# Warm transposes moved to a PSUM bank of their own, and attention's order and engine tables replaced

## The chip, the cores and the metric

The kernel runs on one core of a Trainium2 chip. The metric is the device time of one execution in microseconds (us), as the median of several runs. Five engines work side by side, each through a queue of its own in order: TensorE (PE: matmuls, transposes), VectorE (DVE), ScalarE (ACT), GpSimd (POOL) and SyncE (SP, which issues DMAs).

## The reference

```python
scores = scale * np.matmul(q, k.transpose(0, 1, 3, 2))          # 4 batches x 8 heads, 576 x 576, head size 64
thresh = np.max(scores, axis=-1, keepdims=True) - tau
scores = np.where(scores >= thresh, scores, -1000000000.0)
scores = scores - np.max(scores, axis=-1, keepdims=True)
attn = np.exp(scores)
attn = attn / (np.sum(attn, axis=-1, keepdims=True) + 1e-09)
x = np.matmul(attn, v)                                          # to 2304 tokens x 512
...
x = (sigmoid(x @ w_gate) * (x @ w_val)) @ w_out                 # 512 -> 1536 -> 512
h = x @ w_in                                                    # 512 -> 2048
out = (h * np.cos(h)) @ w_out2
```

## The kernel before

Every fp32 matrix product is made from high and low parts (fp32r), so most operands are first split: a "hi" copy on ACT or POOL, a "lo" difference on DVE or POOL. The program has two stages. The first computes attention and, in between, part of the first MoE layer's products; the second holds the rest of both MoE layers. Its order is in the tables LATER and WHO, which the change does not touch.

Attention goes through 16 pairs of heads, `Pair` p, each with 9 tiles of 128 query rows, `Queries` n (144 tiles). A tile is a chain: **S** (scores, PE, into the PSUM tile `s`, of which there are two), **M** (row minimum of the negated scores, DVE), **E** (exponential, ACT), **Y** (threshold, one value per row, on ACT, POOL or DVE by the table YS), **K** (mask and row sum, DVE, which reads `s` a last time), **T** and **t** (transposes of the result, PE, into `t`), **H**/**h** (hi part, ACT), and the lo part in one of three ways by LOWS and LOWS_L: **L**/**l** (DVE, straight from PSUM), **C** and **G** (ACT copies, POOL subtracts), or **N**/**n** and **O**/**o** (PE subtracts, ACT copies). **V** multiplies with the values; **F** and **A** (ACT, DVE) fold its two halves, and SHARED says which V instead takes more matmuls and needs no fold. The splits of q, k and v are **Q q**, **J j**, **Z z** (capital for hi, small for lo), scaled by **s**; the engine of each, per pair, stands in WHERE, as do **X x** and **U** for attention's result. The twelve weight pieces of the first stage pass through **w** (ACT), **4** and **5** (bit operations on DVE, L516 and L519), **6** (ACT) and **7** (POOL). **P** are the MoE products that fill PE from the fourth pair on.

Who goes when is written out by hand in ORDER: one string of such letters for each engine, which `Plan.put_out` follows letter by letter. A wrong guess in such a string is paid for as a wait, since an engine takes nothing out of turn. `Plan.task` has a flag `alone` for the DVE operations that can't run beside one of POOL.

Before the first tile PE does 42 transposes of the identity into `warm`, a tile of the ring "v" (two PSUM banks, used later by V and P). Between the first tiles it does further groups of four, `filler` (letter **D**), 14 groups by the table FILL, which write a part of the tile's own `s` that nobody reads:

```python
    def filler(s):
        for _ in range(4):
            nc.tensor.transpose(s()[:, 1, HALF:HALF + P], ident, ident)
...
            for _ in range(int(FILL[n])):
                task("PE", 0.43, "D", lambda: filler(s), sc, uses=[s])
```

Of the kernel before, what the change touches and what calls it, by code (L numbers as in the profile page):

```python
# [52 lines left out]

ORDER = dict(
    PE=(
        "SDDSTDSDDDDSTStNnTSNTSDtnDTTSNNNStTDNStTSTVDDtNSSTVBTtSSTTDDNtVSSTTVNNtSTVtSNnSTTNVtSNSBTtSNSTnVTTVNtSnSTTNN"
        "SNtPTPtPSSPVTTPSVPtSTPSBPPtTPSTSPTPStVPTTSSPVNtPNSPTSVtPTTPStVPTPBSPTtPSTPSTtPVSTTVtSSVTtVnSTTPSPtPTPPBSStPP"
        "TPSTSVtTPSPSTTVPtSPTSVtTVTStPSPPTBPStSTPVTTPSStVTPTPSPtSPTPStPVTTSVPtTPBSPStTPPTSPPTStVTPSStTVPSPSVTtVSPTTPP"
        "tSSTPBPtTSSTTVtPSTTVStSTtVnVTSTPStPTPBSPtTPSPTVSSTtVPSSTTPPtPTSPStPTVTSPtSTBPPTPVStSPTPSPTtPSVTTSVtSPTPSVPTt"
        "PSStTVBPTPSSTtPVTPSStTVPTTPSPTPtSPTPVSPttSPTPBSPTVStTVSTTPSPtVTPSStPPTtPSSPTVPTTSSVtPTPSBPTPtSSPTPTPStPSVTTV"  # L60
        "tSSTVtPTTVtPSBTPSPPTStPSTTVStVTPSTPPStPPTPStSVTPTSPtSTVPTBPSTtSPtVTPSSVTTVPStPTPtPPTPTPtVPBBVV"
    ),
    ACT=(
        "JQJQEQHwEYEHEhOEHo6HOEhowEHHHOOOYEhhHEO6hpwCEEHYH6hOsHEERwhCHaaHHYEhE6OFwEHCHHEOOh6hEYHFhpwOoEHYEOYHh6OEREHw"
        "aOhFHCoY6EEHHFahwOoEHHHOOOhhEEH6wehEeFHCEp6HEYehFHERwYYEChHeeEH6HehEYYEFHCwHEYeEHOhOFhp6eHEYhFwCYHeHEh6FHREe"
        "HEYheHCYEhHEXFeHEHHFhhEQHhEYpoaFHCHhEeEHeREEhYCHeHeEEhHCFEeHHEHFphheCHEhHFEHhFCEEYRHheeECHEHHeFhCEYYEFHHHeQE"
        "YYhhEeHhYpeFHHCEFZhECeHREYHChEHeeEChYHYEHFeEYYHEHFhheEFHhEpFECHHheHEREhHCeHEHhFYeEHEHFHhhJHhEYFEoHFpHCEhYHeR"
        "EhHeYEEHeFEEhHFCHHHEEYehhpeHEheEHHFhHCYEeEReCHFEHhYEHhECeEFCHHHEFhHphECEFHhCehHEEFCRHHYYEEhFCHeYhHEEHHHFXsHe"
        "hEhHEepFhhEHeRCEHeEFYhCHEHHFCEheYEFCHhhEEYHeheHHEYEeFpHHCEhFEHReEHCheEEHHeheEEFHCHHhhFpHEhFCHHYhEeRFCHEECHhE"
        "eeHCHFhEFEHHHEehhYeEHChEEYFHHephHEEFHCRHChhYEEHeFEFHCFHHEhhEHYhCpeHHXhFeFbFX"  # L70
    ),
    DVE=(
        "jqjMqKqMLMKKM4MKY5KMLYMK4KM5MKllKMlM4Y5KKIMMYlLYKK4lMML5KKlMM4KA5MlKlKAM4M5KKlMIMYKK45MMAzKLKAM4YKM5MllKKLMM"
        "Yl4KA5MKLIKMlAMLKK4lM5KLMMLlKKAMM4K5lKAMlMLlK4A5ILKlMALYMKLKlMMlKLKMALKLMLAllMKLxKAMLMIlKKLMMKKMlLMKKlMAMKYL"
        "LKLAllMIMKlLAKlMAYMKKLMMYlKKLMMlAKKALLMLMKllMLlKALIMKYAlKMMKzlKMLMlKKLMMAKLKLAllMMYYKALlMYAIKKLlMMLKKlMMLKLl"
        "AMKLKLLllAMMLKAKMLAIMlKLKMLlMYKKLMMAKKlAMMLLLKKllMLIMlYKKLLlAMMKKMYMKLlAKMlMKKMALLYKAlMMlYYIKKAlMMlLYKKAzMML"
        "KKlMMAlLKKLLLAxMLlMKLYlKMYAIllKMMKLMKYlAKMYLAMlKKAMMYllKKLlLMMYLKKAMMLYYIKAlLMKYKMMlYYKLKMLlMKKALLMllAILYlAK"
        "MLlKMAMKKMlMYYKLAMKlKAMLLMLllKKMMlKKLLMAMlLIYKKAMMllYKKLMMAAKLLMAllKKlULILxlxAUAAUxx"
    ),
    POOL=(  # L80
        "YZYzJYjs7cYQqYJ7jG7QqZYGz7YcYGJ7jsQ7YUqZY7XxcUXxYsYG7YQq7GJjY7GscQZGYzJ7qG7UjGYZzYcsxYUXqYYJGYjZYYGzYscQGJYG"
        "YqUZGjYXGczGsUXxxqGGYJGjscGQqZzJjUYXYGYGcYxZUYXxjGYsQzqYYYcsQYqGJZGYzjGsYcYGGUQZGqYGJGjUYcGXxZzYQqJYGUjGGcsZ"
        "XxGQqUXGxzJsGjYYcGQqGYGYGGYZcJjYzYUGZYGGzUYYcGGXXRR"
    ),
    SP=(
        "100W21kkdd0W21sWsssk0kWdd1ssssW0rrssssWdkk2RRdWssssrrWRRk0kWssss12ddgWgg0ddssssWrgg1sssrsWggRRgkDk0ssss2dgrr"
        "ssssRRgggk21kd0gssssDDgkr1rdgssssRg2dRkggssss0grgdrRRsgsssD2ggdg1kkssss0rDrdg2ssssg1gdRRggD2kkdssssrr1RRssss"
        "kggk0dssssggg1rr0sRsgss2dRggdkkDD0ssgrdsskkssssd2rggR1Rssssrr2g0Rksssggks1DddgRssssd0grr2ggRkssssdggRk10dggr"
        "ssDssrgssssggkgd1kR2ssgssRDggDdrssssdk2rRRkgssssggrrssssRRDDDDggg"
    ),  # L90
)
# [1848 lines left out]
```

## Time and profile before

| | |
|---|---|
| median of 3 runs | 1111.09 us (1110.85 to 1112.88) |
| the profiled execution | 1111.66 us |
| its span, first to last instruction | 1109.9 us |
| busy: PE, DVE, ACT, POOL | 97%, 83%, 69%, 54% of the span |
| attention's last products on PE start | 401.18 us |
| granted TensorE clock, mean | 0.998 |

The profiled execution lies 0.6 us above the median, and 1.8 us of it are outside the span. Instructions are listed by engine, source line and the tiles they write and read. Matmuls overlap, so that their durations exceed the distance from one to the next.

### The profile page before, as it was taken

The page shows a single profiled execution, that of the slowest core. Times are in us where ns is not written, and L with a number is a line of the kernel's source. Part 1 is how long each engine was busy: PE and PEld are TensorE (multiplying, and loading weights), DVE is VectorE, ACT ScalarE, POOL GpSimd, SP SyncE. Part 2 cuts the span into 40 slices and gives each one's busy share as a digit, 9 for nine tenths or more (in the row PEclk, how much of TensorE's full clock was granted, in tenths as well). Part 3 has the DMA queues.
Part 4 walks back from the last instruction along what each step waited for, and adds up shares of the span by engine and source line. Part 5 has one row for each costly group of instructions (what it writes and reads, how often), then busy time and mean ns, then how long its engine had stood idle before and what let it go on. Part 6 is the DMA issues. An engine that isn't in the chain of part 4 may idle for free.

```text
span 1109.9 us, 17653 instructions
## 1 busy us (share of the span) xinstructions
PE 1076.6 (97%) x5816; PEld 917.4 (83%) x5816; DVE 926.6 (83%) x1631; ACT 766.7 (69%) x1507; POOL 597.3 (54%) x508
## 2 busy tenths in 40 slices
PE   6889999999999999999999999999999999999998
PEld 6768888888888878987888888888888888888886
DVE  6999998998998856887887655879788899889997
ACT  5889879888888855555654434357876767797774
POOL 4788878878886625432234442244244525445563
PEclk9999999999999999999999999999999999999999
DMA  6657675766666449898876645685444445457752
GB/s 184 158 154 217 193 211 167 199 181 187 182 188 182 125 163 313 303 322 293 292 259 219 200 172 197 219 254 209 157 169 168 152 152 190 173 207 240 279 211 85
DMA packets 88093, 225.53 MB, mean 203 GB/s; under 512 B 14410, under 2 KB 22722, under 8 KB 78274
## 3 DMA queue, kind: packets, MB, share of 16 engines
q1 hardware_dynamic: 87842, 224.08, 63.1%
q8 instruction: 46, 0.75, 0.3%
q10 hardware_dynamic: 160, 0.33, 0.1%
q14 instruction: 45, 0.37, 0.1%
HBM read 150.18 MB, written 59.84 MB: 189 GB/s over the span
## 4 chain that ended last, share of the span: by engine, by line
PE 51%; DVE 1%; DMA 1%; ACT 0%; issue 0%; ACTq 0%
PE h L1391 5%; PE h L1392 5%; PE h L1393 5%; PE h L1580 4%; PE h L1581 4%; PE h L1582 4%; PE o L1700 4%; PE o L1701 4%; PE o L1702 4%; PE o L564 3%; PE o L563 3%; PE o L565 3%; DMA early<-gd 1%; PE o L1791 1%; PE o L1790 1%; PE o L1792 1%
## 5 line engine op out<-in xcount | busy, mean ns | idle before, releaser
L1626 POOL TENSOR_TENSOR g<-raws,g 128x512 fp32r<-128x512 f32 x68 | 94.6, 1400 | 138.1 <-ACT g L1625 115.9
L915 DVE TENSOR_REDUCE sm<-s 128x1 f32<-128x576 f32 x144 | 106.1, 750 | 10.9 <-PE s L909 8.1
L923 DVE SCALAR_TENSOR_TENSOR p<-s,sm,p 128x576 f32<-128x576 f32 x128 | 102.6, 812 | 12.0 <-ACT p L920 7.6
L920 ACT ACTIVATE p<-s,sm 128x576 f32<-128x576 f32 x128 | 94.0, 742 | 15.3 <-DVE sm L915 10.6
L1391 PE MATMUL h<-x,w 128*128 128x256 f32 (+1 forms) x304 | 101.4, 333 | 0.0
L1392 PE MATMUL h<-x,w 128*128 128x256 f32 (+1 forms) x304 | 101.3, 333 | 0.0
L1393 PE MATMUL h<-x,w 128*128 128x256 f32 (+1 forms) x304 | 101.3, 333 | 0.0
L851 ACT ACTIVATE PT<-t 128x512 fp32r<-128x512 f32 (+1 forms) x160 | 86.2, 554 | 21.6 <-PE t L939 18.1
L909 PE MATMUL s<-kk,qh 128*128 128x288 f32 x320 | 92.0, 318 | 9.3 <-DVE p L923 7.8
L1006 PE MATMUL v<-PT,vn 128*128 128x320 f32 (+2 forms) x532 | 84.8, 303 | 3.2 <-DVE x L981 3.2
L1710 DVE TENSOR_TENSOR y<-o,y 128x512 f32<-128x512 f32 x120 | 78.7, 682 | 6.1 <-PE o L1702 5.8
L939 PE MATMUL t<-ident,p 128*128 128x128 f32 x512 | 76.3, 276 | 3.5 <-DVE PT L862 1.9
L1006 PEld LDWEIGHTS v<-PT,vn 128*128 128x128 f32 (+1 forms) x532 | 74.0, 187 | 5.6 <-DVE x L981 4.1
L871 POOL TENSOR_TENSOR PT<-praw,PT 128x512 fp32r<-128x512 f32 x48 | 64.1, 1336 | 26.5 <-ACT praw L866 15.6
L1700 PE MATMUL o<-g,w 128*128 128x512 f32 x196 | 76.7, 392 | 0.5 <-ACT o L1716 0.5
L1701 PE MATMUL o<-g,w 128*128 128x512 f32 x196 | 76.4, 390 | 0.0
L1702 PE MATMUL o<-g,w 128*128 128x512 f32 x196 | 76.3, 389 | 0.0
L909 PEld LDWEIGHTS s<-kk,qh 128*128 128x128 f32 x320 | 58.8, 189 | 21.1 <-DVE p L923 9.9
L1580 PE MATMUL h<-form,w 128*128 128x512 f32 x192 | 75.0, 390 | 0.5 <-ACT side L1549 0.5
L1581 PE MATMUL h<-form,w 128*128 128x512 f32 x192 | 74.8, 389 | 0.0
L1582 PE MATMUL h<-form,w 128*128 128x512 f32 x192 | 74.7, 389 | 0.0
L528 POOL TENSOR_TENSOR w<-wt,w 128x512 fp32r<-128x512 f32 x30 | 39.6, 1325 | 64.5 <-ACT w L524 64.4
(207 smaller groups left out, 3520.2 us busy)
## 6 DMA issues: line engine op xcount, KB each, us to landing
w<-wd SPq DMA_DIRECT2D x62, 1024.0 KB
wd<-stage SPq DMA_DIRECT2D x64, 512.0 KB
gd<-st SPq DMA_DIRECT2D x64, 256.0 KB
wraw<-in_moe_w_out_dram SPq DMA_DIRECT2D x28, 512.0 KB
raw_k<-in_k_dram SPq DMA_DIRECT2D x30, 304.0 KB
raw_q<-in_q_dram SPq DMA_DIRECT2D x30, 288.0 KB
wraw<-in_moe_w_in_dram SPq DMA_DIRECT2D x16, 512.0 KB
spare<-gd SPq DMA_DIRECT2D x7, 1024.0 KB
```

Of the source, the lines that this page charges most:

```text
L909: nc.tensor.matmul(s[:, half, 0:HALF], qq, keys[:, half * HALF:half * HALF + HALF], start=(i == 0), stop=(i == len(mms) - 1),)
L915: nc.vector.tensor_reduce(self.sm()[:, 0:1], self.s()[:, :, 0:HALF], axis=AX.XY, op=ALU.min)
L1006: nc.tensor.matmul(o, w, x, start=z == 0, stop=z == len(steps) - 1)
L1391: nc.tensor.matmul(o, w_hi, x(0, c), start=begin, stop=False, **late)
L1392: nc.tensor.matmul(o, w_hi, x(1, c), start=False, stop=False, **late)
L1393: nc.tensor.matmul(o, w_lo, x(0, c), start=False, stop=c == KC - 1, **late)
L1580: nc.tensor.matmul(ps(), of(0, c), hi, start=fresh and c == 0, stop=False, skip_group_check=True)
L1581: nc.tensor.matmul(ps(), of(0, c), lo, start=False, stop=False, skip_group_check=True)
L1582: nc.tensor.matmul(ps(), of(1, c), hi, start=False, stop=c == 1, skip_group_check=True)
L1700: nc.tensor.matmul(ps(), of(0, c), hi, start=begin, stop=False, skip_group_check=True)
L1701: nc.tensor.matmul(ps(), of(0, c), lo, start=False, stop=False, skip_group_check=True)
L1702: nc.tensor.matmul(ps(), of(1, c), hi, start=False, stop=True, skip_group_check=True)
```

## The change

The `filler` groups no longer write the tile's `s` but `warm`, which becomes a buffer of the ring "v" under the name `spare`; the first V is made to wait for all of them, since `spare` holds one of the ring's two banks until then. FILL has 15 groups instead of 14, all in the first five tiles; the opening block has 36 transposes instead of 42. All of ORDER is replaced, and so are LOWS, LOWS_L, SHARED, WHERE and YS. In counts over the first stage: Y on POOL 55 to 44, on ACT 50 to 38, on DVE 39 to 62; G 48 to 43; L 92 to 96, l 89 to 96; N 20 to 21, n 7 to 0; V without fold 5 to 6; on POOL J 14 to 9, Z 15 to 10, X 12 to 9, j 15 to 14, q 15 to 14, z 13 to 14; what leaves POOL of the hi copies goes to ACT, of the lo parts to DVE.

```diff
 ORDER = dict(
     PE=(
-        "SDDSTDSDDDDSTStNnTSNTSDtnDTTSNNNStTDNStTSTVDDtNSSTVBTt...
+        "SDDDSDSDDTTSNNSDTtDSTSNDDDtTSSTNNNDtDDTDSStNTTVNNtSSTVBT...
...
     DVE=(
-        "jqjMqKqMLMKKM4MKY5KMLYMK4KM5MKllKMlM4Y5KKIMMYlLYKK4lMML5...
+        "jqMjqKqMMKK45MMYYKKlMMYLKKlMM4q5lKKlMlM4j5KKMMlILYKKMl4M...
...
 FILL = (
-    "223002001 200002000 000000000 000000000 000000000 000000000 000000000 000000000 "
+    "444120000 000000000 000000000 000000000 000000000 000000000 000000000 000000000 "
...
     warm = ps_v.tile([P, 512], F32, tag="v", name="warm", bufs=2)
-    for _ in range(42):
+    for _ in range(36):
         nc.tensor.transpose(warm[:, 0:P], ident, ident)
...
-    def filler(s):
+    spare = buf("v", lambda: warm, 2, any_order=True)
+    fills = []
+
+    def filler():
 
         for _ in range(4):
-            nc.tensor.transpose(s()[:, 1, HALF:HALF + P], ident, ident)
+            nc.tensor.transpose(spare()[:, 0:P], ident, ident)
...
-                task("PE", 0.43, "D", lambda: filler(s), sc, uses=[s])
+                fills.append(task("PE", 0.43, "D", filler, sc, uses=[spare]))
...
-                      *lasts, pair.v_done, pvs[0], uses=[bank, self.PT, self.LZ, pair.vb])
+                      *lasts, pair.v_done, pvs[0], *(fills if pvs[0] is None else []), uses=[bank, self.PT, self.LZ, pair.vb])
```

How the instructions stand at two places. First PE's queue at the start of the program, before: `warm` is the opening block, `s` the scores, `s<-ident` the filler groups, `t` the transposes of a finished tile.

```order
L597 MATMUL warm<-ident 128x128 x42
L909 MATMUL s<-kk,qh_99 128x288
L909 MATMUL s<-kk,ql_101 128x288
...
L777 MATMUL s<-ident 128x128 x8
L909 MATMUL s<-kk,qh_99 128x288
L909 MATMUL s<-kk,ql_101 128x288
...
L939 MATMUL t<-ident,p 128x128 x4
L777 MATMUL s<-ident 128x128 x4
L909 MATMUL s<-kk,qh_99 128x288
```

The same place of the changed kernel:

```order
L598 MATMUL warm<-ident 128x128 x36
L913 MATMUL s<-kk,qh_99 128x288
L913 MATMUL s<-kk,ql_101 128x288
...
L781 MATMUL warm<-ident 128x128 x12
L913 MATMUL s<-kk,qh_99 128x288
L913 MATMUL s<-kk,ql_101 128x288
...
L781 MATMUL warm<-ident 128x128 x4
L913 MATMUL s<-kk,qh_99 128x288
L913 MATMUL s<-kk,ql_101 128x288
```

The filler groups write another tile than the scores, and the first tile's transposes move behind the third tile's scores.

Second, DVE's queue around the third weight piece, before (`sm<-s` is M, `p,sums<-s,sm,p` is K, `wt<-wraw` is 4, `wt<-we,wt` is 5, `LT<-t,LT` is l, and `sm<-sm,taus` is Y):

```order
L915 TENSOR_REDUCE sm<-s 128x1
L862 TENSOR_TENSOR LT<-t,LT 128x128
L915 TENSOR_REDUCE sm<-s 128x1
L516 TENSOR_SCALAR wt<-wraw 128x512
L772 TENSOR_SCALAR sm<-sm,taus 128x1
L519 SCALAR_TENSOR_TENSOR wt<-we,wt 128x512
L923 SCALAR_TENSOR_TENSOR p,sums<-s,sm,p 128x576 x2
```

and in the changed kernel:

```order
L866 TENSOR_TENSOR LT<-t,LT 128x128
L919 TENSOR_REDUCE sm<-s 128x1
L517 TENSOR_SCALAR wt<-wraw 128x512
L686 TENSOR_TENSOR kk<-raw_k,kk 64x1216
L520 SCALAR_TENSOR_TENSOR wt<-we,wt 128x512
L927 SCALAR_TENSOR_TENSOR p,sums<-s,sm,p 128x576 x2
L919 TENSOR_REDUCE sm<-s 128x1 x2
```

The lo part of a pair's keys, which POOL did at this place, now stands on DVE between 4 and 5 (and one piece earlier the lo part of a pair's queries does). Both M's ahead of the piece and both K's behind it keep their place.

## Rows read from the trace of the kernel before

**Rows 1.** Busy time by stretch: PE, PEld, DVE, ACT, POOL, clock, DMA, GB/s
```profile
20.00:127.00 107.00, 92.99 (x593) 78.19 (x592) 101.29 (x192) 91.22 (x207) 91.25 (x76) 0.98 0.67 182
127.00:402.00 275.00, 268.98 (x1761) 237.03 (x1761) 247.22 (x558) 228.54 (x507) 211.58 (x205) 1.00 0.62 173
402.00:1110.00 708.00, 700.37 (x3372) 589.32 (x3370) 568.24 (x864) 438.12 (x782) 288.06 (x212) 1.00 0.63 219
```

**Rows 2.** PE's waits up to 127 us: total, times, longest
```profile
PE s L909 <- DVE p L923: 5.9, 6, 2.4
```

**Rows 3.** Source lines 516 and 519 on DVE: shortest, median, longest in ns
```profile
L516 DVE TENSOR_SCALAR wt<-wraw x12: 417/806/2721, 20.2 to 117.8; 128x512 uint32<-128x512 uint32 x12
...
L519 DVE SCALAR_TENSOR_TENSOR wt<-we,wt x12: 671/1148/2973, 22.1 to 120.1; 128x512 uint32<-128x512 uint32 x12
```

**Rows 4.** Timeline at the third weight piece: start, duration; idle before it
```profile
37.15 2.79 POOL L685 TENSOR_TENSOR kk<-raw_k,kk 64x1216 fp32r<-64x1216 f32 x1
...
37.50 2.72 DVE L516 TENSOR_SCALAR wt<-wraw 128x512 uint32<-128x512 uint32 x1
...
42.69 0.40 PE L909 MATMUL s<-kk,qh 128*128 128x288 f32 x1 [2.40 <-DVE p L923]
```

**Rows 5.** Busy time of the stretch behind that wait, columns as in rows 1
```profile
42.60:46.40 3.80, 3.71 (x17) 3.66 (x18) 2.86 (x10) 2.51 (x5) 3.16 (x3) 0.56 0.96 264
```

**Rows 6.** Source line 777, the filler: who waited for it
```profile
  ACT p L920: 3.7, 3
  DVE p L923: 1.5, 1
```

**Rows 7.** Timeline of the first three tiles
```profile
1.36 6.81 PE L597 MATMUL warm<-ident 128*128 128x128 f32 x42 [1.36 <-POOL halfpi L476]
...
6.77 0.35 DVE L683 SCALAR_TENSOR_TENSOR ql<-raw_q,taus,qh 128x128 fp32r<-128x128 f32 x1
...
7.92 0.38 PE L909 MATMUL s<-kk,qh 128*128 128x288 f32 x1
...
8.74 0.76 DVE L915 TENSOR_REDUCE sm<-s 128x1 f32<-128x576 f32 x1 [0.83 <-PE s L909]
...
9.53 0.82 DVE L683 SCALAR_TENSOR_TENSOR ql<-raw_q,taus,qh 128x576 fp32r<-128x576 f32 x1
...
10.24 0.74 ACT L920 ACTIVATE p<-s,sm 128x576 f32<-128x576 f32 x1 [1.78 <-PE s L777]
...
11.83 0.82 DVE L923 SCALAR_TENSOR_TENSOR p<-s,sm,p 128x576 f32<-128x576 f32 x1 [1.48 <-PE s L777]
...
12.57 0.68 DVE L683 SCALAR_TENSOR_TENSOR ql<-raw_q,taus,qh 128x448 fp32r<-128x448 f32 x1
...
14.39 0.38 PE L909 MATMUL s<-kk,qh 128*128 128x288 f32 x1
...
18.79 0.82 DVE L923 SCALAR_TENSOR_TENSOR p<-s,sm,p 128x576 f32<-128x576 f32 x1 [1.23 <-ACT p L920]
```

**Rows 8.** Groups by line and shape, 5 to 127 us: busy, mean ns, idle before
```profile
L519 DVE SCALAR_TENSOR_TENSOR wt<-we,wt 128x512 uint32<-128x512 uint32 x12 | 16.7, 1390 | 0.1
L516 DVE TENSOR_SCALAR wt<-wraw 128x512 uint32<-128x512 uint32 x12 | 13.0, 1082 | 0.0
L862 DVE TENSOR_TENSOR PT<-t,PT 128x512 fp32r<-128x512 f32 x14 | 9.6, 683 | 0.9 <-ACT PT L851 0.7
...
L862 DVE TENSOR_TENSOR LT<-t,LT 128x128 fp32r<-128x128 f32 x11 | 3.1, 280 | 0.0
...
L685 DVE TENSOR_TENSOR vn<-raw_v,vn 128x640 fp32r<-128x640 f32 x1 | 1.8, 1824 | 0.0
...
L1006 PE MATMUL v<-PT,vn 128*128 128x320 f32 x52 | 9.0, 316 | 1.2 <-DVE x L981 1.2
```

**Rows 9.** Source line 772, the thresholds on DVE: columns as in rows 3
```profile
L772 DVE TENSOR_SCALAR sm<-sm,taus x39: 145/206/218, 21.9 to 381.5; 128x1 f32<-128x1 f32 x39
```

**Rows 10.** PE's waits over the whole span
```profile
PE o L564 <- DVE g L1364: 1.9, 1, 1.9
```

More of the change, by code (lines that the diff above doesn't have):

```diff
@@ L55 @@
     PE=(
[L56 to L60, printed above, removed]
@@ L61 @@
-        "tSSTVtPTTVtPSBTPSPPTStPSTTVStVTPSTPPStPPTPStSVTPTSPtSTVPTBPSTtSPtVTPSSVTTVPStPTPtPPTPTPtVPBBVV"
+        "SDDDSDSDDTTSNNSDTtDSTSNDDDtTSSTNNNDtDDTDSStNTTVNNtSSTVBTStNSTTSNtVSTVSNTStTVtTSNSTtNSBTVtSSTVTTStVTTSNNNSTtP"
+        "PPSTSPtNVTStSVPTPBPStPPSTSPPTTPStVTPSPTtSVPSTPStVPTTPStVPTBPSTStPTPTPSStPVSTTVSNtNSVTtVSTTPSPtTPSBPPtTPSSTPT"
+        "PVtTSSTPtVPSTtSPTPTVtSPSTBPVtTPSSPPTTPStSVTTVSPtTPPStPTSVPTStPVSTBPSPPtTPSSTPTPtVSSTPTPtVSVTPtSPSTTPVPtTSSBP"
+        "TtPPSTTVtSPSTTVSNSTtVTVStStPTPPBTPSPtTSPVSSTTVPTtPSSPTtPPSSTPtVTPSTPtSVPBTSPPTPStSTTVPtTPSStTVPSTPtSPVTTPStS"
@@ L62 @@
+        "VTBPSPtTSPTPTVSStTVPTPSPtTSPtPTVPTSStPTPBPSPStVTVSSTPTPtVTSSPtTPPTPSStPTPTSVPTtPSSVPBTStPTPSTPtPTPSSVTVStPTS"
+        "tVTPTSVtTPSBPPTtPSSTTVStTVPStTPSPTPPStPSTTVPTtPSSBTVPStTPSTtPVPSSVTVPTtPSPTPPtPTPVPtTVBBV"
     ),
     ACT=(
-        "JQJQEQHwEYEHEhOEHo6HOEhowEHHHOOOYEhhHEO6hpwCEEHYH6hOsHEERwhCHaaHHYEhE6OFwEHCHHEOOh6hEYHFhpwOoEHYEOYHh6OEREHw"
-        "aOhFHCoY6EEHHFahwOoEHHHOOOhhEEH6wehEeFHCEp6HEYehFHERwYYEChHeeEH6HehEYYEFHCwHEYeEHOhOFhp6eHEYhFwCYHeHEh6FHREe"
-        "HEYheHCYEhHEXFeHEHHFhhEQHhEYpoaFHCHhEeEHeREEhYCHeHeEEhHCFEeHHEHFphheCHEhHFEHhFCEEYRHheeECHEHHeFhCEYYEFHHHeQE"
@@ L67 @@
[L67 to L70, printed above, removed]
+        "JQJQEYQZYEEwHHOOEE6hHHOEEhQwHHYHOEOhOhE6HhOwpYHHEEO6OshHEEYHRwhOYEHHaaE6OhEYwHEF6aHHOEhhHEQhHwpOEHh6OEERHhFw"
@@ new lines @@
+        "aCHYEFHH6EhYEwaHHHOOOYHhEEh6ewHEhEYOFeHhpJYFEER6ehHEweCHEYeHHEh6eEFwCHeHhEh6HYEFJehHEpFwCHHe6hEECHFRHhEYeEHZ"
+        "HehEECeFHEHHFpOhhOEYHFhYEFHHCYEehZHEREJHeheHEECHehFCHEEHhhHFeCHhEEHeYHhFpHEReECFHhEEYCHeHheEFHHCHFEhHhYEehpe"
+        "EYHFEXHEheCFRHYEEhHCeeHEEHYCheFHEEYHhheHFJEFhHCeHHpEEehCHFREHhEYeHEHChFeEEHHHFOYHEEhhHaCFphhHEEeHRehHEECeFHH"
+        "ZEEFheHCEEhHeHhpHEehFHEHeEhFRHEECHheHHEEFChHeEYhhHHEFChEHpYEHFeHhCEEHCRJFHCEhEHHFeEhHEXFHHXhhHeEhEHpFeCHhYEE"
+        "YZRHeeEEYhCFHFHHEEheCHFEhHHEYeCheHhpEHEHeXEFCeHhEFRHEheHJHEEhCeeEEFHHpHFhhHhCEFHeCHEYFhCHREYEHheeEHHCEFhEHFH"
@@ L71 @@
+        "hHEhYeHEZheEpHCHEYFhHCeREECHhHFYhEEHeFFCEHFHEHhhCEHpehHXehFHXFFbX"
     ),
     DVE=(
[L73 to L76, printed above, removed]
@@ L77 @@
-        "KKlMMAlLKKLLLAxMLlMKLYlKMYAIllKMMKLMKYlAKMYLAMlKKAMMYllKKLlLMMYLKKAMMLYYIKAlLMKYKMMlYYKLKMLlMKKALLMllAILYlAK"
-        "MLlKMAMKKMlMYYKLAMKlKAMLLMLllKKMMlKKLLMAMlLIYKKAMMllYKKLMMAAKLLMAllKKlULILxlxAUAAUxx"
+        "jqMjqKqMMKK45MMYYKKlMMYLKKlMM4q5lKKlMlM4j5KKMMlILYKKMl4MKLY5KMlMK45KAMLLMlYlYLKKlM4I5KlMMYYKKLAl4M5MKLMLKlA4"
+        "UKMM5LYKlKMlM4lKKAMLMl5IAKYKMYLKl4MM5KLLMlYKKAM45MKLLlKlAMMLlYKA45MLIlYKKAMLMlYKKLMMlKYKMALKMAlIlMKLAlKMLAKl"
+        "MMLYKKLlMMLYzKKlAMMYYKKLLllMMAlKLKlLAIMMLYKKAMMYlKKxMYLlMAKLLAMKllLKlMMKLYAMKLIYlKMAMKYKlMMLKKlMMALYKKLLlAMl"
@@ L79 @@
+        "KlAMMYLLKKIlMMAYKLlKMLYKlMAMKKLLMMALYKlKlxMlMAYlILKKLMlMYYKKMAMYLLKKAlMMYKKLLllMMLKlALIKMLlKMAYLMKYKlMMLLKKl"
+        "AMMKLLlYlKMAMlYKIKLAMMYlKKMMAYlYKKLLMMAlYLKKLLMlAlLMYKlYKILMlMAKKLMMKKAlMMYALLKKMlAMYLLKKllMMYlKLLMKYKAMxlYI"
+        "KMALYlKMLMLYKKlMMYKKALLllAMlMYKLAIMKAlMKKLMlMKLMYAKlLAKMLLlMlKLKMlMIYKLKlAMMYKKzMlLAMlYKKLMAMYYAKALLMlKlKILl"
+        "xlLAAxxUAUx"
     ),
     POOL=(
-        "YZYzJYjs7cYQqYJ7jG7QqZYGz7YcYGJ7jsQ7YUqZY7XxcUXxYsYG7YQq7GJjY7GscQZGYzJ7qG7UjGYZzYcsxYUXqYYJGYjZYYGzYscQGJYG"
@@ L82 @@
-        "YqUZGjYXGczGsUXxxqGGYJGjscGQqZzJjUYXYGYGcYxZUYXxjGYsQzqYYYcsQYqGJZGYzjGsYcYGGUQZGqYGJGjUYcGXxZzYQqJYGUjGGcsZ"
-        "XxGQqUXGxzJsGjYYcGQqGYGYGGYZcJjYzYUGZYGGzUYYcGGXXRR"
-    ),
-    SP=(
[L86 to L89, printed above, removed]
+        "zYJjsY7cY7YJ7QqZz7YcJs7jYq7UZGXYx7cXxsz7YQqj7ZYscGz7YGQq7GY7UjGcYzXGYxUXxsQGqYjYGcsGQJYqUGYZjXGGczsYJUQqxGjG"
@@ new lines @@
+        "sGYcGQZzYqGYZjUGzYGYcXJxUXGsYQjqYzGcJYGsYYQqYjZzYYGcsGQqUGYGGjGYZcUxxzsJGQqYjUXGYscQGzUYqGxYGjZcYzGGsYGUJQGY"
+        "qcYGjYzGGYZcGUGUYGRRX"
+    ),
+    SP=(
+        "1002W1kkdd0W1sssWs0k2Wkdd1ssssW0ssssWrr2ddRRkkWssssrrkWdRR0Wssss1kg2dW0gsrgsssWg1sgsssWdrggkkd2RRg0ssdrsrsgg"
+        "RRssssDDg2g1dkksssgs0rggr1ssdssRkRgg2kds0grrsgssd1ggsRRksssDggDDkd0sdssrgs21rgssssg2kgDgRkdgdRssssrr1RssssR0"
+        "kg2dggsssskggrr1RR0gssssdgdgkD2skgsss0g1ddssssrgk2k0rsgsssRrR1DssrgssgkRD2kDdgsRsssdg0rrggddRRkkgssss1g2g0ds"
+        "sgsrdgsgrRsssskkRgg1ssssDDDg2dgssssgrdrkgg2ssRksRrsrssssRRggDDggD"
@@ L94 @@
 LOWS = (
-    "VTTVTTTGT VGVTGTTTT TGVTTTVGV VGVVGTVGV VVGVVVVGV VGVGVVGVG VGVGVVVVG GGVGVVVGV "
-    "VGVVVVVVG VVVGVVVVV GGVGGVGGV GVGVVVVVG VGVGGVVGV VGVVGVVGV GGVGVVGVV VGGVGVGVV "
+    "TTTVTTTTT VTVTTVVTT VGVVTTVTV VGVVGVVGV GVVGVTVGV VVVGGVGVV VGGVGVVVV GGVGVVGVV "
+    "GVVGTVVGV VGVVGVVVV VGVVGVGVG GGVVVVVVG VGVVGVGVV GVVVGVGVG GVGVVVVVG GGVVGVGVV "
 ).replace(" ", "")
 LOWS_L = (
-    "TTVV VVTV TTVV VVVV VVTV VVVV VVVV VVVV VVTV VVVV VVVV VVVV VVVV VVVV VVVV VVVV "
+    "VVVV VVVV VVVV VVVV VVVV VVVV VVVV VVVV VVVV VVVV VVVV VVVV VVVV VVVV VVVV VVVV "
 ).replace(" ", "")
@@ L109 @@
 SHARED = (
-    "SS.. S..S .... .... S... .... .... .... .... .... .... .... .... .... .... .... "
+    "SS.S S..S .... .... .... .... .... .... S... .... .... .... .... .... .... .... "
 ).replace(" ", "")
 WHERE = dict(
-    Q="APPPPPAPAPPPPPPP", q="DPPPPPPPPPPPPPPP", J="APPPPPPPPPAPPPPP", j="DPPPPPPPPPPPPPPP",
-    Z="PPPPPPPAPPPPPPPP", z="PPDPPPPDPPPDPPPP", s="APAPPPPPPPPPPAPP", X="PPAPPPPPPAPPPPAA", x="PPPDPPPPPDPPDDDD", U="PPPPPPPPPPPPPPDP",
+    Q="AAPAPPPPPPPPPPPP", q="DDPPPPPPPPPPPPPP", J="APPPAAAPPAPPAPAP", j="DPDPPPPPPPPPPPPP",
+    Z="APPPAAPPPAPPAPAP", z="PPPPPDPPPPPPPPPD", s="APAPPPPPPPPPPPPP", X="PPPPPAPPAAPAAPAA", x="PPPPDPPDPPPDDDDD", U="PDPPPPPPPPPPPPPP",
 )
 YS = (
-    "PPAPDDPAP DADDAPPPA AADPAPDPP DPAAAPAAA PAADAAPPP APPPAPPPD PPDADPAAA AADAPAAAA "
-    "DDDPPPAPP AAPADPPPA PDAPDAPPD DDPDAAAPP DDPADDADA DADDDDDPP DAPPDDPAP PAPDADPPA "
+    "AAPDDDPAP PADAADAPD DPDDAPAAD PAADDAPDP ADPDADPDP AAADPDPDD PAPDDADPA ADDADPADA "
+    "PDPDADPPA DDPDDDPDP PPPDDPPAD DAPDDDPDD DAAPADPDA DPDDDPDDP DPAAPDPAP DAPDADDDP "
 ).replace(" ", "")
```

## The prediction

> **What bounds the kernel now.** I read the busy times by stretch first. From 402 us on PE is busy for 700.4 of 708 us, and the change touches nothing there. From 127 to 402 it is busy for 269.0 of 275, so 6.0 us at most can be won, while DVE has 27.8 us idle. Only the head is another thing: from 20 to 127 us PE is idle for 14.0 of 107 us, DVE for 5.7, ACT and POOL for some 16 each [rows 1]. The reader is to see that DVE sets the pace of the head: what PE waits for most there is the mask K [rows 2].
>
> The next view is that of single lines on DVE. The two bit operations of a weight piece, 4 and 5, take at least 0.417 and 0.671 us, but half of them are above 0.806 and 1.148, and the longest take 2.7 and 3.0 [rows 3]. The timeline shows why: at 37.50 operation 4 starts 0.35 us after POOL's lo part of the keys and ends 0.28 us after it. Behind the held DVE stand the two K's, PE runs dry, and its next scores start after 2.40 us of idleness [rows 4]; then the granted clock is 0.56, near the lower of its two levels (1.2 of 2.4 GHz), until 46.4 [rows 5]. Operation by operation, with the shortest as the price of the work itself, the 24 of them contain 12 x (1.390 - 0.671) + 12 x (1.082 - 0.417) = 8.6 + 8.0 = 16.6 us in which DVE was only held up [rows 3, 8].
>
> The third view is the start. The filler groups write the tile `s`, so each waits for the tile's last reader, and the tile's next reader waits for it: E for 3.7 us in all and K for 1.5 [rows 6].
>
> **The filler.** A walk through the first three tiles, with the durations of the timeline [rows 7]. The 42 opening transposes take 7.92 - 1.36 = 6.56 us, 0.156 each; 36 end at 6.98. The lo part of the queries is done at 7.12, so S of tile 0 starts near 7.15 instead of 7.92, and M ends at about 8.75 instead of 9.50. E now waits for M alone and ends near 9.6 instead of 10.98. K is behind the two lo parts that DVE has left (0.76 and 0.82 after M), so it runs from about 10.3 to 11.1 instead of 11.83 to 12.65; the next lo part (0.68) ends near 11.75, and S of tile 2 starts there, where it now starts at 14.39: a gain of 2.6. M of tiles 1 and 2, their E and K (0.76, 0.74, 0.82 each) then follow without a filler between them, and K of tile 2 ends near 15.1; it now ends at 19.61. That is 4.5 us. I take 3.5 of it, since right behind these K's DVE has the first 4 and 5, which POOL's lo part of the second pair's keys (2.79 [rows 4]) may hold, and since a copy of the values on ACT now stands in front of tile 1's E and waits for its load. At the least I take 1.5, at the most 4.5.
>
> On PE itself the filler costs nothing but its own time: four transposes more, six fewer at the start. Its bank is free to take, since the first V stands behind the last group in PE's string.
>
> **The engine tables, up to the 40th K** (the last one before 127 us; the letters are counted in the strings). DVE gets 6 more Y at 0.206 [rows 9], 1.2; 5 more L at 0.683 and 5 more l at 0.280, 3.4 + 1.4 [rows 8]; one lo part of queries and one of keys, 1152 and 1216 columns. DVE's own of 448 and 576 columns take 0.68 and 0.82 [rows 7], 1.1 ns a column, which makes 1.45 + 1.5; and one multiplication of 576 columns, 0.8 as the lo part of that width. It loses one lo part of the values (1.82 [rows 8]), one M that comes later (0.76), and two A, whose price I put between l and L, 0.45 each. Together 9.75 - 3.5 = +6.3 us on the engine that sets the pace.
>
> POOL loses five G, five Y, and with the hi copies some 15 us in the same part of the strings, so it is in DVE's way less often. The operations that can be held are 27 instead of 24. If each were held as now, they would lose 18.7; if each stood where POOL is idle, nothing. The new order puts them side by side (4, q, 5 and 4, j, 5), which is one chance to collide in place of two. I take half of today's loss away, 8.3 of 16.6; the bounds are -2 and 16.6.
>
> **The rest of the first stage.** Behind the 40th K DVE gets 17 more Y (3.5 us) and about nothing else; the cover is its 27.8 idle us, and without it they would cost 3.5. ACT's load is level. PE does five more products for one more V without fold, at 9.0/52 = 0.173 each [rows 8], +0.9, with the corrections N and n about level. Since PE is full here, what the head gains is handed on whole.
>
> **The second stage** keeps its instructions. One wait of 1.9 us in it hangs on a load [rows 10] and could grow or go; I count 0, with 2 either way.
>
> **The sum:** -3.5 + 6.3 - 8.3 + 0.9 = -4.6 us against the profiled execution's 1111.66 us, or 1107.1; it lies 0.6 above the median of the runs, so 1106.5 on their scale.
>
> **A rule against the change.** The 39 thresholds on DVE last at most 0.218 us, also while POOL works, which it does for most of that time [rows 1, 9]. So the 23 more of them cost their own time and no lock. The Trainium skill's page "SBUF — State Buffer", section "Who interferes with whom", says that DVE's tensor_scalar can enter a mode that takes the port pair shared with GpSimd, and that the later of the two then waits for the whole instruction of the other. Operation 4 is a tensor_scalar and agrees, the threshold is one too and does not. By the rule taken for every tensor_scalar, the 23 thresholds would be held like operation 4.
>
> **Rivals.** (a) The held time moves and does not shrink: other operations meet POOL's long ones, the new q and j on DVE among them. With nothing saved the sum is -3.5 + 6.3 + 0.9 = +3.7, 1114.8: slower. It decides where less than 1.5 us of the 16.6 is saved. For it: the added DVE work alone outweighs the filler, and DVE has only 5.7 us idle in the head. Against it: POOL's smaller load. (b) The thresholds are held too, at operation 4's mean of 0.665: 23 x 0.665 = 15.3, of which the six in the head, 4.0, have no cover; +3.7 + 4.0 gives 1118.8. Rows 9 speak against it. (c) The saving is small, 1.5 to 5.9 us, and pays for the added work: 1109 to 1113, centre 1111. Here too belongs that the start is limited by its loads and the filler's waits were slack. (d) Nearly all of the held time goes, the gap before 42.69 and the low clock with it, and PE loses 2 of its 6 idle us later: -4.5 + 6.3 - 15 + 0.9 - 2 = -14.3, 1096.8. Against it: ACT's own 91 of 107 busy us in the head [rows 1] would soon be the limit. A larger gap on PE, since the filler no longer waits and so bunches right behind the scores, would show as a second stretch like that of rows 5, whose 3.8 us at a clock of 0.56 cost 3.8 x 0.44 = 1.7; it stays inside these ranges.
>
> **How the numbers follow.** The forecast has 0.53 (own range 1102 to 1109), (a) 0.14, (b) 0.02, (c) 0.16, (d) 0.15. About 0.2%, 2.2 us, is what a measurement can tell from no change, so faster means under 1108.9: 0.68; same 0.16, slower 0.16. The range from 1097.5 to 1115 leaves out the upper half of (a), (b) and the far half of (d), some 2 in 10.
>
> **What would show it.** Right: no wait for the filler on ACT or DVE, and tile 2's K ending before 16 us; 4 and 5 with a summed excess near 8 us; DVE's work in the head larger, the 40th K near 121 us where it now ends just before 127, and the last PE instruction of attention near 396. Wrong: an excess near 16 us, on 4 and 5 or on the new q and j; a K count that runs level with the old one at 40 us; a second stage whose length differs from 708 us by more than 2.

## The result and the profile after

The changed kernel takes 1096.76 us (1096.58 to 1102.01 in 4 runs), the kernel before 1111.99 us beside it: a ratio of 0.9874 [0.9842, 0.9906]. Timed again (experiment 10) it gave 0.9892 [0.9873, 0.9911]. So the change wins 12 to 14 us, where the forecast had 4.6. On the scale of the 1111.09 us shown ahead the two ratios are 1097.1 and 1099.1 us; the median itself lies 0.7 us below the range, and some 5 us below the 1102 to 1109 that the forecast gave itself. Of the rivals it is (d), with 1096.8, that came nearest.

The profiled execution takes 1096.72 us, 14.94 less than that of before. Its span and the busy times, from the page:

```profile
span 1094.9 us, 17669 instructions
...
PE 1073.1 (98%) x5813; PEld 915.7 (84%) x5813; DVE 916.9 (84%) x1666; ACT 771.5 (70%) x1496; POOL 567.5 (52%) x478
```

The ends of the n-th mask K, read from the two timelines, show where the time went (us):

| K | before | after | difference |
|---|---|---|---|
| 3 (tile 2) | 19.6 | 15.1 | -4.5 |
| 11 | 43.4 | 37.6 | -5.8 |
| 15 | 54.5 | 47.3 | -7.2 |
| 25 | 84.0 | 73.3 | -10.7 |
| 30 | 95.9 | 90.0 | -5.9 |
| 40 | 126.5 | 115.2 | -11.3 |
| 144 | 392.7 | 380.6 | -12.1 |
| end of attention on PE | 401.7 | 388.6 | -13.1 |

Three steps, and one back: 4.5 us in the first three tiles, 6 us from there to the 25th K, a loss of 4.8 between the 25th and the 30th that is soon made good, and little afterwards. Now the views. First the busy times by stretch of the changed kernel, columns as in [rows 1]; the first line reaches to the 40th K, the other two split at the end of attention:

```profile
0.00:115.20 115.20, 101.47 (x669) 87.75 (x669) 104.11 (x224) 99.28 (x208) 75.75 (x76) 1.00 0.72 197
115.20:388.60 273.40, 271.18 (x1775) 238.33 (x1773) 246.42 (x578) 232.10 (x504) 205.22 (x191) 1.00 0.64 179
388.60:1094.90 706.30, 700.47 (x3372) 589.58 (x3372) 566.42 (x865) 440.08 (x784) 286.53 (x212) 1.00 0.63 218
```

The kernel before, up to its own 40th K:

```profile
0.00:126.50 126.50, 106.80 (x684) 90.65 (x684) 110.65 (x210) 99.53 (x220) 97.17 (x92) 0.99 0.67 181
```

In the head DVE is busy for 104.1 of 115.2 us, so it still sets the pace there, but it needs less time: it was busy for 110.65 of 126.5. The clock is 1.00 in every stretch. Behind the head PE is idle for 2.2 us, where it was for 6.0. Next the groups of DVE between 5 and 116 us, columns as in [rows 8]:

```profile
L520 DVE SCALAR_TENSOR_TENSOR wt<-we,wt 128x512 uint32<-128x512 uint32 x12 | 12.2, 1020 | 0.5
L517 DVE TENSOR_SCALAR wt<-wraw 128x512 uint32<-128x512 uint32 x12 | 5.9, 492 | 0.0
L686 DVE TENSOR_TENSOR kk<-raw_k,kk 64x1216 fp32r<-64x1216 f32 x1 | 1.4, 1423 | 0.0
L686 DVE TENSOR_TENSOR ql<-raw_q,qh 128x1152 fp32r<-128x1152 f32 x1 | 1.4, 1351 | 0.0
```

The same 24 operations 4 and 5, with the same shortest durations taken off as in the prediction, now hold 12 x (1.020 - 0.671) + 12 x (0.492 - 0.417) = 4.2 + 0.9 = 5.1 us of waiting, instead of 16.6. The lo parts of keys and queries that came to DVE take 1.42 and 1.35, no more than their columns cost.

The start, in the timeline of the changed kernel (start, duration, the idle time before it):

```profile
1.36 6.23 PE L598 MATMUL warm<-ident 128*128 128x128 f32 x36 [1.36 <-POOL halfpi L477]
...
7.35 0.38 PE L913 MATMUL s<-kk,qh 128*128 128x288 f32 x1
...
8.16 0.76 DVE L919 TENSOR_REDUCE sm<-s 128x1 f32<-128x576 f32 x1 [1.01 <-PE s L913]
...
8.96 0.74 ACT L924 ACTIVATE p<-s,sm 128x576 f32<-128x576 f32 x1 [0.35 <-DVE sm L919]
...
10.47 0.81 DVE L927 SCALAR_TENSOR_TENSOR p<-s,sm,p 128x576 f32<-128x576 f32 x1
...
11.21 0.68 DVE L684 SCALAR_TENSOR_TENSOR ql<-raw_q,taus,qh 128x448 fp32r<-128x448 f32 x1
...
11.79 1.56 POOL L686 TENSOR_TENSOR vn<-raw_v,vn 128x640 fp32r<-128x640 f32 x1 [9.87 <-ACT vn L669]
...
14.29 0.81 DVE L927 SCALAR_TENSOR_TENSOR p<-s,sm,p 128x576 f32<-128x576 f32 x1
```

E follows M without the filler between them (it waited 1.78 us for it in [rows 7]), K stands behind DVE's own lo parts only, and tile 2's K ends at 15.1. The filler's line, asked who waited for it, gives one entry where [rows 6] had 5.2 us of ACT and DVE:

```profile
  PEld t L943: 0.2, 1
```

### The profile page after: what moved, and what is told of

Read it like the earlier page. It is cut to its first block, busy times and chain, and to the rows that moved or that the text cites. A ratio compares the mean times of both kernels' runs of the same rounds, so it can differ in the third digit from the quotient of the medians.

```text
span 1094.9 us, 17669 instructions
## 1 busy us (share of the span) xinstructions
PE 1073.1 (98%) x5813; PEld 915.7 (84%) x5813; DVE 916.9 (84%) x1666; ACT 771.5 (70%) x1496; POOL 567.5 (52%) x478
## 4 chain that ended last, share of the span: by engine, by line
PE 85%; DVE 7%; ACT 4%; DMA 1%; issue 1%; POOL 0%; SPq 0%; DVEq 0%; ACTq 0%; POOLq 0%
PE h L1395 7%; PE h L1396 7%; PE h L1397 7%; PE s L913 6%; PE v L1010 5%; PE o L564 5%; PE o L565 5%; PE o L566 5%; PE h L1584 4%; PE h L1586 4%; PE h L1585 4%; PE t L943 4%; PE o L1704 4%; PE o L1705 4%; PE o L1706 4%; PE m L564 2%
## 5 line engine op out<-in xcount | busy, mean ns | idle before, releaser
L855 ACT ACTIVATE PT<-t 128x512 fp32r<-128x512 f32 (+1 forms) x160 | 86.5, 555 | 16.5 <-PE t L943 13.2
L1629 ACT ACTIVATE g<-raws 128x512 fp32r<-128x512 f32 x106 | 64.3, 624 | 13.1 <-DVE raws L1672 8.3
```

## The experiments

Each was timed beside the kernel before; a ratio below is against that. Where a gap to the changed kernel is given, it is the difference of the ratios times 1111 us, against its two timings, 0.9874 and 0.9892; experiments 11 and 12 are set beside experiment 10 by their medians too, since the three ran on one chip.

**1. Only the bank.** The old tables, with the filler in the bank of its own; the old FILL's four late groups, behind the first V, are dropped.

```diff
-    "223002001 200002000 000000000 ...
+    "223002001 000000000 000000000 ...
-            nc.tensor.transpose(s()[:, 1, HALF:HALF + P], ident, ident)
+            nc.tensor.transpose(spare()[:, 0:P], ident, ident)
```

> The kernel before with its own tables, only the filler moved to the bank of its own; the four groups that stood behind the first V are dropped, since the bank has to be free there. If the filler's place in the score tile was worth what the walk through the first tiles says, 2 to 4 us faster than before (1108 to 1110), with no wait of ACT or DVE on the filler and the third tile's K ending 2 us or more before 19.6. If the waits were slack under the old order, under 1 us and the K's level with before at 40 us.

It took 1107.20 us, 0.9966 [0.9954, 0.9978]: 3.8 us won. The 3rd K ends at 16.2 and the 11th 3.2 us earlier than before, and the offset stays to the end of attention (398.5). 4 and 5 are held for 16.5 us, as before, and the clock still falls, to 0.58 between 32 and 36 us and 0.64 between 40 and 44. So what the start wins is handed on whole, and no more than that comes from the bank under the old tables.

**2. No filler in the old kernel.** FILL all zero, the letter D out of PE's string.

```diff
-    "223002001 200002000 000000000 ...
+    "000000000 000000000 000000000 ...
```

> The kernel before without any filler group. If the filler only cost waits, as fast as the run with the bank of its own or up to 1 us faster. If PE needs it for its clock, stretches with a granted clock near 0.5 appear before 40 us and 1 to 4 us of the gain are lost.

1107.77 us, 0.9973 [0.9961, 0.9985]: as good as moving it. In the old order the filler cost about what its bank saves, though without it the clock falls early (0.60 between 12 and 20 us). Against experiment 1 it is 0.8 us longer by the ratios, inside both intervals, so the low clock shows no clear price here.

**3. One weight piece moved in the old order.** In DVE's string 4 and 5 of the third piece go behind the two masks that they held up in [rows 4].

```diff
-        "...KKlMlM4Y5KKIMM...
+        "...KKlMlMYKK45IMM...
```

> The kernel before with one edit in DVE's string: the third weight piece's operations 4 and 5 behind the two K's instead of in front. They were held for 2.3 and 0.9 us by POOL there, and PE stood for 2.4 us. If held time on DVE is paid in full in the head, 2 to 3.5 us faster than before (1108 to 1110), no gap at 42 us and no low clock there. If the head has slack elsewhere, or the hold only moves to the next piece, within 1 us of before.

1109.79 us, 0.9996 [0.9986, 1.0005]: nothing won. The profile says where it went. The masks of the place do come sooner, but 5 comes later, and with it ACT's w, which waits for it; ACT takes nothing out of turn, so its copies behind w are late, and PE waits for one. Timeline of this kernel:

```profile
39.43 2.79 POOL L685 TENSOR_TENSOR kk<-raw_k,kk 64x1216 fp32r<-64x1216 f32 x1
...
42.61 1.66 DVE L519 SCALAR_TENSOR_TENSOR wt<-we,wt 128x512 uint32<-128x512 uint32 x1
...
44.30 0.63 ACT L524 ACTIVATE w<-wt 128x512 fp32r<-128x512 f32 x1 [2.44 <-DVE wt L519]
...
45.64 0.97 PE L939 MATMUL t<-ident,p 128*128 128x128 f32 x4 [1.96 <-ACT PT L858]
...
48.05 2.66 POOL L685 TENSOR_TENSOR ql<-raw_q,qh 128x1152 fp32r<-128x1152 f32 x1
...
49.47 1.52 DVE L516 TENSOR_SCALAR wt<-wraw 128x512 uint32<-128x512 uint32 x1
```

The reader is to see the chain 5, w, PT, t, and that the next piece's 4 then runs into POOL's lo part of the queries and is held to 1.52 us. The 11th K ends at 42.2, earlier than before, the 15th at 56.2, later. Part of this is the execution and not the edit: it took 1112.21 us, the longest of the ten, its clock was 0.50 from 12 to 20 us (see the last section), and its 3rd K, which stands ahead of the edit, already ends at 21.9, 2.3 us later than before. Against that K the 11th comes 3.4 us sooner than before and the 15th 0.6, so most of what the edit wins is lost again within four tiles.

**4. POOL's lo parts cut short, old kernel.** POOL computes the lo parts of q and k on an eighth of the columns only; the rest of these low parts is left out of the result.

```diff
+    nc.gpsimd.memset(f32(qls[1]), 0.0)
...
+                if engine != "DVE":
+                    part = slice(0, KW // 8)
...
+            if nm == "q" and engine != "DVE":
+                to, hi, raw = (x[:, :, 0:S // 8] for x in (to, hi, raw))
```

> The kernel before, with POOL's lo parts of queries and keys on an eighth of their columns (the rest of those low parts is left out), so that POOL's longest operations last some 0.4 us instead of 2.7 to 2.8; DVE's work is unchanged. If DVE held up by POOL is most of what the changed kernel won, the summed excess of operations 4 and 5 falls from 16.6 us to under 7 and the time by 7 to 11 us (1101 to 1105). If the order of the work, and not the hold, was the limit, under 3 us.

1099.51 us, 0.9893 [0.9877, 0.991]: 11 to 12 us by median and ratio, with DVE's order untouched. The groups of DVE between 5 and 127 us:

```profile
L519 DVE SCALAR_TENSOR_TENSOR wt<-we,wt 128x512 uint32<-128x512 uint32 x12 | 10.1, 840 | 0.1
L516 DVE TENSOR_SCALAR wt<-wraw 128x512 uint32<-128x512 uint32 x12 | 6.4, 533 | 0.0
```

The held time falls from 16.6 to 2.0 + 1.4 = 3.4 us, and the time by most of that. The 40th K ends at 117.8. POOL's own work shrinks by the same edit, which could be a cause of its own. But in the kernel before no engine is seen to wait for POOL's lo parts up to 127 us: behind the first 2 us the one wait of another engine that is put on POOL is 1.2 us, for a threshold. Held time on DVE in the head is therefore paid nearly one to one.

**5. The same in the changed kernel.** The edit of experiment 4.

> The changed kernel, with POOL's lo parts of queries and keys on an eighth of their columns (the rest left out). Its operations 4 and 5 are held 4.8 us in all. If the hold is what the two kernels differ by, it gains 1.5 to 4 us, much less than the kernel before does by the same edit. If the edit speeds both kernels up by the same amount, POOL's load and not the place of 4 and 5 is what counts.

1095.48 us, 0.9858 [0.9842, 0.9874], 2 to 4 us below the changed kernel; by the profile 5.1 us of held time become 2.1 + 0.7 = 2.8. What the new order left to win there is small.

**6. The bank and the short lo parts together, old tables.** The edits of experiments 1 and 4.

> The kernel before with both: the filler in a bank of its own (four late groups dropped), and POOL's lo parts of queries and keys on an eighth of their columns (the rest left out); the old tables. The two alone took 3.7 and 11.4 us. If DVE held by POOL and the filler's waits are two causes and all there is, 1095 to 1097, within 2 us of the changed kernel with the short lo parts. If the new order wins by something else, it stays above 1099.

1094.88 us, 0.9852 [0.9835, 0.9869]; the 40th K ends at 111.9, attention at 385.3. The two causes, the start and the held time, are enough for the whole gain. It goes 2 to 4 us further than the changed kernel, which has 5 us more work on DVE in the head and keeps 5.1 us of held time.

**7. The new tables without the bank.** The filler writes the tile `s` again, 15 groups at the same places of PE's string, each into the tile whose S stands ahead of it.

```diff
-    "444120000 000000000 ...
+    "312020304 000000000 ...
-            nc.tensor.transpose(spare()[:, 0:P], ident, ident)
+            nc.tensor.transpose(s()[:, 1, HALF:HALF + P], ident, ident)
```

> The changed kernel with its new tables, but the filler groups write the score tile again (each group the tile whose scores stand in front of it). If the bank of its own is worth what the start shows, 2.5 to 4.5 us slower than the changed kernel (1099 to 1101) with the third tile's K later than 15.1 by as much. If the new order gains by itself, under 1 us slower.

1106.44 us, 0.9953 [0.9938, 0.9968]: 7 to 9 us above the changed kernel, where 2.5 to 4.5 was expected. The filler's source line here, what it waited for and who waited for it (us, times):

```profile
  DVE sm L916: 9.7, 8
  ACT p L921: 2.9, 4
...
  ACT p L921: 6.0, 4
  DVE p L924: 0.6, 1
```

The filler waits 12.6 us for readers of the tiles, and E waits 6.0 us for the filler. The 3rd K ends at 21.0.

**8. The new tables without any filler.** FILL all zero, D out of PE's string; the 36 opening transposes stay.

```diff
-    "444120000 000000000 ...
+    "000000000 000000000 ...
```

> The changed kernel without any filler group. If they are idle weight, within 1 us of it (1096 to 1097). If they hold TensorE's clock up, stretches near 0.5 appear before 40 us and it is 1 to 4 us slower.

1104.09 us, 0.9932 [0.9917, 0.9947]: 4 to 6 us above the changed kernel. The busy times between 8 and 30 us, columns as in [rows 1], of the changed kernel:

```profile
8.00:30.00 22.00, 18.48 (x133) 15.49 (x131) 20.42 (x40) 18.18 (x37) 10.96 (x10) 1.00 0.70 192
```

of the one without filler:

```profile
8.00:30.00 22.00, 13.99 (x62) 11.23 (x60) 18.50 (x32) 13.20 (x24) 9.56 (x9) 0.77 0.61 160
```

and of experiment 7:

```profile
8.00:30.00 22.00, 15.01 (x87) 13.33 (x88) 15.63 (x28) 11.23 (x21) 7.97 (x7) 0.77 0.59 159
```

The filler in its own bank keeps PE busy for 18.5 of the 22 us and the granted clock at full; without it, or with waits between its groups, the clock is 0.77 on the mean, with stretches at 0.50, the lower of its two levels. DVE is busy for 18.5 and 15.6 us there instead of 20.4. But the clock is not all that differs in the profile of the kernel without filler. Its timeline:

```profile
1.36 6.90 PE L598 MATMUL warm<-ident 128*128 128x128 f32 x36 [1.36 <-POOL halfpi L477]
...
8.01 0.38 PE L913 MATMUL s<-kk,qh 128*128 128x288 f32 x1
...
11.82 1.54 POOL L686 TENSOR_TENSOR vn<-raw_v,vn 128x640 fp32r<-128x640 f32 x1 [9.91 <-ACT vn L669]
...
11.88 1.95 DVE L684 SCALAR_TENSOR_TENSOR ql<-raw_q,taus,qh 128x448 fp32r<-128x448 f32 x1
...
17.42 3.05 POOL L686 TENSOR_TENSOR kk<-raw_k,kk 64x1216 fp32r<-64x1216 f32 x1
...
17.93 3.09 DVE L520 SCALAR_TENSOR_TENSOR wt<-we,wt 128x512 uint32<-128x512 uint32 x1
```

The 36 opening transposes, which stand ahead of any filler, took 6.90 us in this execution and 6.23 in the first profile of the changed kernel. So the scores start at 8.01 instead of 7.35, and two operations of DVE start just behind POOL's and are held, by 1.3 and 2.4 us. Experiment 12, which has all its filler, meets the same two holds, and the two profiles are alike: the 11th K ends at 43.4 here and 42.6 there, 4 and 5 are held for 6.6 and 6.7 us, and the executions take 1104.20 and 1104.24 us. What the missing filler itself costs is therefore not shown by this run.

**9. Two pieces moved in the changed order.** In DVE's string 5 of the first piece goes behind an M, and 5 of the ninth behind the mask and threshold that it holds up.

```diff
-        "jqMjqKqMMKK45MMYYKKl...
+        "jqMjqKqMMKK4M5MYYKKl...
-        "UKMM5LYKlKMlM4lKKAMLMl5IAKYKMYLKl...
+        "UKMM5LYKlKMlM4lKKAMLMlIAKY5KMYLKl...
```

> The changed kernel with two edits in DVE's string: the ninth piece's operation 5, held 2.4 us by POOL's keys, goes behind the next inverse, A, K and Y, and the first piece's 5, held 0.8, behind one M. If held time is still paid in full, 1.5 to 3 us faster than the changed kernel (1094 to 1095). If PE is the limit there already, within 0.7 us.

1098.53 us (1095.02 to 1100.39), 0.9878 [0.9857, 0.9899]: no difference from the changed kernel. In its profile the 11th K ends 3.2 us later and the stretch from the 25th to the 30th is 2.7 us shorter (14.0 for 16.7), so a gain and a loss, which the next runs take apart.

**10. The changed kernel again**, timed on the chip of the next two and of experiment 6.

> The changed kernel once more, on the chip of the next three, so that they have it beside them: 1096 to 1098 us.

1099.02 us (1097.14 to 1102.69), 0.9892 [0.9873, 0.9911]. Its profiled execution takes 1097.14, the 11th K ends at 36.5, attention at 389.0.

**11. Only the ninth piece moved.** The second line of experiment 9. The place in the changed kernel's timeline:

```profile
85.22 2.78 POOL L686 TENSOR_TENSOR kk<-raw_k,kk 64x1216 fp32r<-64x1216 f32 x1 [1.30 <-ACT kk L669]
...
85.45 3.10 DVE L520 SCALAR_TENSOR_TENSOR wt<-we,wt 128x512 uint32<-128x512 uint32 x1
...
89.16 0.82 DVE L927 SCALAR_TENSOR_TENSOR p<-s,sm,p 128x576 f32<-128x576 f32 x1
```

5 starts 0.23 us after POOL's lo part and is held for 2.4, in the stretch from the 25th to the 30th K.

> The changed kernel with the ninth piece's operation 5 alone behind the inverse, A, K and Y. In the run with two edits this stretch (25th to 30th K) was 2.7 us shorter, while the first edit cost 3 us at the start. If both are what they look like, 2 to 3 us faster than the changed kernel. If the gain was given back later, as it was where one piece was moved in the kernel before, within 0.7 us of it.

```profile
89.58 2.81 POOL L686 TENSOR_TENSOR kk<-raw_k,kk 64x1216 fp32r<-64x1216 f32 x1 [1.31 <-ACT kk L669]
...
90.83 0.82 DVE L927 SCALAR_TENSOR_TENSOR p<-s,sm,p 128x576 f32<-128x576 f32 x1 [0.34 <-ACT p L924]
...
91.70 1.24 DVE L520 SCALAR_TENSOR_TENSOR wt<-we,wt 128x512 uint32<-128x512 uint32 x1
```

In its own timeline, above, a mask runs first and 5 is held for 0.6. The stretch takes 14.0 us for 16.7, so this hold is 2.7 of the 4.8 us lost there; the kernel before needs 11.9, and the rest isn't traced. 1095.43 us (1094.79 to 1099.86), 0.9856 [0.9837, 0.9874]: by the medians 3.6 us below the changed kernel on the same chip, by intervals that just touch. The profiled execution is its longest. From the 25th K to the end of attention it takes 313.9 us (experiment 9: 313.7), the changed kernel 315.2 and 316.7 in its two profiles: a gain of 1 to 3 us. It is the fastest form of the changed kernel with a full result.

**12. The opening block at its old length.** The changed kernel with 42 opening transposes for 36.

```diff
-    for _ in range(36):
+    for _ in range(42):
```

> The changed kernel with 42 opening transposes instead of 36. If the first scores wait for the opening block, they start near 7.9 instead of 7.35 us and the kernel is 0.4 to 0.7 us slower. If loads or the split of q and k set the start, no difference.

1103.40 us (1100.94 to 1104.24), 0.9925 [0.9909, 0.994]: 4.4 us above the changed kernel on the same chip by the medians, 3.7 by the ratios, where 0.4 to 0.7 was expected. The scores start at 8.10, only 0.8 and 1.2 us later than in the two profiles of the changed kernel (7.35 and 6.92). The timeline of this kernel:

```profile
11.90 1.54 POOL L686 TENSOR_TENSOR vn<-raw_v,vn 128x640 fp32r<-128x640 f32 x1 [9.98 <-ACT vn L669]
...
11.96 1.96 DVE L684 SCALAR_TENSOR_TENSOR ql<-raw_q,taus,qh 128x448 fp32r<-128x448 f32 x1
...
17.20 2.92 POOL L686 TENSOR_TENSOR kk<-raw_k,kk 64x1216 fp32r<-64x1216 f32 x1
...
17.60 3.08 DVE L520 SCALAR_TENSOR_TENSOR wt<-we,wt 128x512 uint32<-128x512 uint32 x1
```

and of the changed kernel in experiment 10:

```profile
10.96 0.68 DVE L684 SCALAR_TENSOR_TENSOR ql<-raw_q,taus,qh 128x448 fp32r<-128x448 f32 x1
...
11.91 1.58 POOL L686 TENSOR_TENSOR vn<-raw_v,vn 128x640 fp32r<-128x640 f32 x1 [10.00 <-ACT vn L669]
...
15.31 0.69 DVE L520 SCALAR_TENSOR_TENSOR wt<-we,wt 128x512 uint32<-128x512 uint32 x1
...
17.17 2.78 POOL L686 TENSOR_TENSOR kk<-raw_k,kk 64x1216 fp32r<-64x1216 f32 x1
```

POOL's lo part of the values starts at 11.9 in both, after a wait of 10 us for ACT's copy, which in experiment 10 waits 0.91 us for the load and here stands behind ACT's copy of the queries. DVE's lo part starts 0.06 us behind it here and 0.95 ahead of it there: 1.96 us against 0.68. That puts the first 5 behind POOL's lo part of the keys as well, 3.08 against 0.69, and the clock falls to 0.79 between 20 and 28 us. The 11th K ends 6.1 us later. The Trainium skill's page "SBUF — State Buffer", section "Who interferes with whom", says that the order of issue decides which of the two engines waits. Here the engine that starts second, DVE, waits, with 0.06 us between the starts; in experiment 10 the two don't overlap.

The same race is lost in the profiles of experiments 9 and 11 (POOL at 11.07 and 11.08, DVE at 11.09 and 11.14), where ACT's copy of the values doesn't wait for its load and starts 0.7 us sooner than in the changed kernel's first profile, and in that of experiment 8, where the opening block takes longer. In experiments 9 and 11 the instructions up to there are those of the changed kernel, so it can lose the race too; that this is what spreads its runs over 1096.6 to 1102.7 us is argued, since none of its longer runs was profiled.

## Why the forecast was right in sign and small by two thirds

**The start: right, and discounted for nothing.** The walk gave 4.5 us and tile 2's K at 15.1; both came out to the tenth in the profiled execution. The tenth is luck: experiment 10's profile has 14.9, and experiments 9 and 11, with the same instructions up to there, 16.3. Of the 1.0 taken off for POOL's lo part in the way, 0.8 came true behind this K, since the first 5 takes 1.49 us for 0.671; experiment 12 shows a risk of more than 1.0. With the old tables the start alone is worth 3.8 (experiment 1).

**The held time: the right mechanism, the term that was mis-sized.** "I take half of today's loss away, 8.3 of 16.6": 11.5 went. The prediction named POOL's smaller load and the pairs put side by side, had no row for how the starts would meet, and took half. POOL is busy for 75.75 us up to the 40th K now, against 97.17, and most of the 24 start where it is not in the way: the ninth piece's 5 alone carries 2.4 of the 5.1 us that are left. Experiments 4 to 6 show this term to be the main one.

**The added work on DVE: right.** Busy time without the held part goes from 94.0 to 99.0 us up to the 40th K: +5.0, where +6.3 was forecast. The moved lo parts take 1.35 and 1.42 where 1.45 and 1.5 were taken, the multiplication 0.74 for 0.8.

**What the filler does for PE: left out, and not settled.** "On PE itself the filler costs nothing but its own time" left out what it may give: between 8 and 30 us the clock is 1.00 in the changed kernel and 0.77 in the profiles of experiments 7 and 8. This is not what made the forecast small, since the clock of the kernel before is 1.00 in that stretch too. Nor do the 4 to 9 us of the two experiments show what the clock is worth: experiment 8's profile has the two holds of experiment 12 and its length, experiment 7 has waits for the filler, and in the old order no filler and a free-running one differ by no more than the noise (experiments 1 and 2). The parts do not add: the bank alone gives 3.8 us, the tables alone (experiment 7) 5, together 12 to 14. Which of the waits, the holds and the clock makes up the rest stays open.

**Up to the 40th K** the sum is then: DVE busy 104.1 for 110.65, that is -11.5 + 5.0, and DVE idle 11.1 for 15.85, -4.8, of which the first three tiles are 3.7: -11.3, where -5.5 was forecast.

**The rest: +0.9 forecast, -1.8 measured in attention, -1.9 behind it.** PE's idle time from the 40th K to the end of attention falls from 6.0 to 2.2 us, the part of rival (d) that had 2 of it. The 1.9 of the second stage is the size of the wait of [rows 10], which the waits of the changed kernel no longer have. The profiles of experiments 1 and 3, with the old tables, don't have it either, and in all the others the stage takes 706.0 to 707.8 us, against 708.2 before and 706.3 after: as far as this shows, the wait went by chance and not by the change.

**The rivals.** (a) fell: the hold shrank, though the ninth piece and the race of experiment 12 show how it moves. (b) fell: the thresholds' source line reads

```profile
L773 DVE TENSOR_SCALAR sm<-sm,taus x62: 146/204/217, 18.3 to 373.2; 128x1 f32<-128x1 f32 x62
```

62 of them and none above 0.217 us, as in [rows 9]; taken for every tensor_scalar, the rule that the prediction weighed doesn't hold here. (c) fell. (d) gives the right time from parts that are partly others: it took 15 of held time where 11.5 went, and nothing in the second stage. The reason against it, that ACT would be the limit, was wrong: ACT is busy for 99.3 of 115.2 us and DVE for 104.1.

**Open.** How much of experiment 7's 7 to 9 us is the clock, how much the filler's waits and how much held time; what the filler in its own bank is worth against none under the new tables, without the two holds; what spreads the changed kernel's runs.
